# Third up projection wholly in seven products: its sums of weights formed earlier, and joint score visits for two more pairs

## The chip, the cores and the metric

The kernel runs on one core of a Trainium2 chip. The metric is the device time of one execution in microseconds. Before the change three runs gave 1011.73, 1011.96 and 1013.79 us; the median, 1011.96 us, is the number to compare with. Engines are called PE (TensorE, matmul), DVE (VectorE), ACT (ScalarE), POOL (GpSimd) and SP (SyncE, which here only issues DMAs).

## The reference

Sliding-window attention with a linear distance bias over 8 batches of 8 heads, 576 positions, 64 columns per head, then a bilinear feed-forward block over all 4608 tokens:

```
scores = q k^T / 8 - slope_h * |i - j|      (kept where 0 <= i - j < 128)
x      = softmax(scores) v                  (576 x 512 per batch)
out    = ((x w_a) * (x w_b)) w_out          (w_a, w_b: 512 x 1536, w_out: 1536 x 512)
```

All inputs are float32. The kernel forms most products from float16 pairs, a high and a low part, with three matmuls (high*high, high*low, low*high) per product.

## The kernel before

**Stages.** The work goes batch by batch. For each of the 8 batches there is an up projection (both w_a and w_b, and the product of the two) and a down projection (w_out). They are called here up 1, down 1, up 2, down 2, ... up 8, down 8; in the code batches count from 0, so up 3 belongs to `b == 2`. An up has twelve blocks of 128 hidden columns (`f` = 0..11), each for both halves of 288 tokens; a down has 2 halves by 4 blocks of output columns, each summed over the twelve `f`.

**Two ways of an up block.** `up_plain` needs 8 products per block, each of 6 matmuls of 288 columns: 48 matmuls. `up_fast` is a Strassen-like scheme with 7 products, 42 matmuls, but more additions: ACT copies and scales (L845, L857, L863), DVE adds and multiplies (L852, L868, L873, L880), and one multiplication on POOL (L875). It also needs other operands: sums and differences of the four weight quarters of a block (slots 3 to 6 of `wup[:, f]`), and sums of the four quarters of x (`split_x` with `fast`). Slot 3 is read by the plain way and overwritten by the sums, so a block's sums can only be formed once the last plain use of that block has been read.

**Sums of weights.** `sums_of_weights(f)` has two steps per block, 24 in all. A step is five POOL additions (L239 to L243), one ACT cast (L244) and one DVE subtraction (L245). Its two temporaries come from the pool of tiles `t` with 4 buffers, which the scores use as well. `ways` says which blocks of which batch are plain or fast, and `quota` lays the 24 steps along the matmul steps of ups and downs: `(8, 48, 6)` puts six of them evenly between step 8 and step 48 of that stage.

**Attention beside it.** While batch b goes through up and down, `attention()` works on the four head pairs of the following batch, a generator whose places (`yield i + k / 7`) are spread by `Pace` over the steps of up and down. `i` counts pairs, `p` is the pair in its batch. For a pair PE forms scores in four PSUM banks (`scores(o, bi)`: L362 float32 for the second batch, L366 float16 pairs later), DVE takes bias and minimum (L370), ACT the exponential (L371), ACT and DVE write normalised probabilities as high and low parts (L383, L384), a DMA transposes them (L389), and PE multiplies by v (L485). `two` says how many banks are formed in the pair's first visit. The next pair's q and k are loaded (L299, L300), squared on ACT (L309), scaled to a high part on ACT (L326) and a low part on DVE (L327), and laid out by four copies on the SP queue (L335 to L338). At `p == 1` the next v is loaded (L256) and squared on ACT (L265). At `p == 0` `split_x` splits the finished x of the batch into high and low parts (L419 on ACT, L420 on DVE), with four subtractions on POOL where the fast way is to be used (L433 to L443).

**What sets the order.** From up 2 on PE follows the order written in the program; DVE, ACT, POOL and the SP queue follow a scheduler that simulates the kernel while it is built and sets each engine's order by it. In up 1 and down 1 only SP keeps the written order, and PE is ordered by the scheduler too. Once built, every engine runs its list strictly in order: an instruction that waits holds up all behind it.

Of the kernel before, what the change touches and what calls it, by code (L numbers as in the profile page):

```python
# [21 lines left out]
B, H, S, D = 8, 8, 576, 64  # L22
# [24 lines left out]
def attention_then_bilinear_ffn(ctx: ExitStack, tc: tile.TileContext, qT, kT, vP, w_a, w_b, w_out, rel, slopes2, outT):  # L47
# [255 lines left out]
    def qk_squares(b, p, qk):  # L303
        o = State()
        o.b, o.p, o.qk = b, p, qk
        sums = small.tile([P, 1], F32, tag="qs", name="qs")
        hi = work.tile([P, 2, S], F16, tag="qkh", name="qkh", bufs=2)
        lo = work.tile([P, 2, S], F16, tag="qkl", name="qkl", bufs=2)
        act.activation(lo.bitcast(BF16), qk, AF.Square, accum_out=sums)  # L309

        o.both = small.tile([P, 2], BF16, tag="both", name="both")
        vec.tensor_scalar(out=o.both, in0=halves, scalar1=sums, scalar2=None, op0=ALU.mult)
        o.kh, o.kl = hi, lo
        return o

    def split_qk(o):

        b, p, qk, hi, lo = o.b, o.p, o.qk, o.kh, o.kl
        tot = ps_at.tile([P, 512], F32, tag="at", name="qtot")
        pe.matmul(tot[:, 0:2], ones16, o.both, start=True, stop=True)  # L320
        sc = small.tile([P, 2], F32, tag="sc", name="sc")
        power_scale(sc, tot[:, 0:2], 1.01, 15)
        own = small.tile([P, 3], F32, tag="own", name="own")
        vec.tensor_tensor_reduce(out=own[:, 0:2], in0=sc, in1=halves, scale=1.0, scalar=0.0, op0=ALU.mult, op1=ALU.add, accum_out=own[:, 2:3])
        own = own[:, 2:3]
        act.activation(hi, qk, AF.Copy, scale=own)  # L326
        vec.scalar_tensor_tensor(out=lo.rearrange("p h s -> p (h s)"), in0=qk.rearrange("p h s -> p (h s)"), scalar=own, in1=hi.rearrange("p h s -> p (h s)"), op0=ALU.mult, op1=ALU.subtract)  # L327
        o.sc = sc

    def lay_out_qk(o):  # L330


        b, p, hi, lo, sc = o.b, o.p, o.kh, o.kl, o.sc
        o.qs = work.tile([P, 2, S], F16, tag="qst", name="qst", bufs=1)
        sp.dma_start(o.qs[0:64, :, :], hi[0:64, :, :])  # L335
        sp.dma_start(o.qs[64:128, :, :], lo[0:64, :, :])
        sp.dma_start(hi[0:64, :, :], hi[64:128, :, :])
        sp.dma_start(lo[0:64, :, :], lo[64:128, :, :])  # L338

        t = small.tile([P, 1], F32, tag="ninv", name="ninv")  # L340
        vec.scalar_tensor_tensor(out=t, in0=sc[:, 0:1], scalar=-8.0, in1=sc[:, 1:2], op0=ALU.mult, op1=ALU.mult)
        o.neg = small.tile([P, 1], F32, tag="neg", name="neg")
        vec.reciprocal(o.neg, t)
        return t

    def before_scores(o, ninv):
        o.bias = work.tile([P, WIN], F32, tag="bias", name="bias")
        pool.tensor_scalar(out=o.bias, in0=rel_sb, scalar1=ninv, scalar2=sl2_sb[:, o.p:o.p + 1], op0=ALU.mult, op1=ALU.mult)  # L348
        o.mn, o.sm, o.rin = (small.tile([P, 9], F32, tag=tag, name=tag) for tag in ("mn", "sm", "rin"))
        o.n, o.parts = 0, []  # L350
# [67 lines left out]
    def split(n, src):  # L418
        act.copy(xs[:, n, 0, :, :], src)  # L419
        vec.tensor_tensor(out=xs[:, n, 1, :, :], in0=src, in1=xs[:, n, 0, :, :], op=ALU.subtract)  # L420

    def split_x(st, plain, fast):

        b11, b12, b21, b22 = (st.v[:, k:k + 2, t:t + HT] for k in (0, 2) for t in (0, HT))
        split(0, b11)
        if plain:
            split(1, b21)
            split(2, b22)
            split(B12, b12)
        if not fast:  # L430
            return
        yield
        pool.tensor_tensor(out=b11, in0=b12, in1=b11, op=ALU.subtract)  # L433
        if not plain:
            split(2, b22)
        pool.tensor_tensor(out=b12, in0=b22, in1=b12, op=ALU.subtract)
        split(4, b11)
        pool.tensor_tensor(out=b22, in0=b22, in1=b11, op=ALU.subtract)
        yield
        if not plain:  # L440
            split(1, b21)
        split(6, b12)
        pool.tensor_tensor(out=b21, in0=b21, in1=b22, op=ALU.subtract)  # L443
        yield
        split(5, b22)
        split(3, b21)
        yield
# [194 lines left out]
    def attention():  # L642


        n = NPAIR * (B - 1)
        qks = {}

        def load(i):
            if i < n:

                qks[i] = (load_plain_qk if i < NPAIR else load_qk)(1 + i // NPAIR, i % NPAIR)

        def squares(i):
            if i >= n:
                return None
            qk = qks.pop(i)
            return qk if i < NPAIR else qk_squares(1 + i // NPAIR, i % NPAIR, qk)

        def split(o):
            if o and o.b > 1:  # L660
                split_qk(o)

        def lay_out(o):
            if o:
                before_scores(o, lay_out_qk(o) if o.b > 1 else -8.0)

        def behind():

            return tc.issue_after(last_read[0].ins) if last_read[0] else ExitStack()

        load(0)
        st, prev = load_v(1), None
        o = squares(0)
        lay_out(o)
        load(1)
        yield 0
        for i in range(n + 1):
            b, p = 1 + i // NPAIR, i % NPAIR

            two = 2 if o and o.b >= 2 else 1  # L680
            for bi in range(two if o else 0):
                scores(o, bi)
            with behind():
                nxt = squares(i + 1)
            if p == 1 and b > 1:
                st = load_v(b)
            if p == 2:
                v_scale(st)
            yield i + 1 / 7
            if o and two == 1:  # L690
                scores(o, 1)

            if p == 2:

                with tc.issue_after(first_reads[0].ins) if first_reads[0] else ExitStack():
                    late.vhl = split_v(st, late.p)
            elif prev and p != 1:
                prev.vhl = split_v(st, prev.p)
            yield i + 2 / 7
            if p == 2:  # L700
                pv(late.p, st, late, late.vhl)
                transpose_probs(prev)
                split(nxt)
            if o and p != 2:
                with behind():
                    normalize(o)
            if p != 2:
                split(nxt)
            yield i + 3 / 7
            if o:  # L710
                scores(o, 2)
            if prev and p not in (1, 2):
                pv(prev.p, st, prev, prev.vhl)
            if two == 2 and p in (1, 3):
                if p == 2:
                    with behind():
                        normalize(o)
                scores(o, 3)
            yield i + 4 / 7
            if p == 2:  # L720
                prev.vhl = split_v(st, prev.p)
                if two == 1 or p not in (1, 3):
                    with behind():
                        normalize(o)
            if o and (two == 1 or p not in (1, 3)):
                scores(o, 3)
            lay_out(nxt)
            load(i + 2)
            if p == 1:
                v_squares(st, (0, 1))  # L730
            if prev and p == 0:
                states[b - 1] = st
                assert started["down"] == b - 2
                for k, _ in enumerate(split_x(st, b - 1 <= 2, b - 1 >= 2)):
                    yield i + (4.2 + 0.2 * k) / 7
            yield i + 5 / 7
            if o:
                with behind():
                    normalize(o)
            if p == 1:  # L740
                v_squares(st, (2, 3))
            yield i + 6 / 7
            if prev and p == 0:
                hidden_scale(st)
            if p == 2:
                pv(prev.p, st, prev, prev.vhl)
            if p == 1:
                late = prev
            elif o:
                transpose_probs(o)  # L750
            prev, o = o, nxt
            yield i + 1
# [221 lines left out]


    every = list(range(NF))
    ways = [(every, [])] * 2 + [(every[6:], every[:6])] + [([], every)] * (B - 3)
    att = Pace(attention())
    spread = chain.from_iterable(sums_of_weights(f) for f in every)

    quota = [((), ()), (((8, 48, 6),), ((0, 48, 4),)), (((0, 24, 2), (28, 66, 3)), ((0, 48, 3),)), (((0, 48, 6),), ())] + [((), ())] * (B - 4)

    def first_batch():
        st = states[0]
# [60 lines left out]
```

## Time and profile before

| | |
|---|---|
| time, median of 3 runs | 1011.96 us |
| the profiled execution: its own time / its span | 1013.37 us / 1011.6 us |
| PE busy | 969.4 us, 96% |
| DVE busy | 681.8 us, 67% |
| ACT busy | 643.0 us, 64% |
| POOL busy | 305.9 us, 30% |
| chain that ended last | PE 60%, DVE 12%, DMA 6%, ACT 6% |

Stages of the span, by the start of the first matmul of each: up 1 from 56 us, up 2 from 212.9, down 2 from 294.5, up 3 from 336.5, down 3 from 417.3, up 4 from 458.8, down 4 from 535.2, up 5 from 576.0, down 5 from 648.5, up 6 from 689.3 to 760.8 us.

How to read it: "busy" is the time in which an engine had an instruction under way. PE is pipelined, and a matmul of 288 columns stands in the trace with some 286 ns though one starts every 123 ns, so PE's idle time, and how long a stage takes, say more than its busy share. Idle time of an engine that PE doesn't wait for costs nothing.

### The profile page before, as it was taken

To read this page: it belongs to the slowest core of one execution; us is meant where nothing else is said; L and a number is where in the kernel's file an instruction comes from. 1 tells how busy PE (TensorE), PEld (TensorE's weight loads), DVE (VectorE), ACT (ScalarE), POOL (GpSimd) and SP (SyncE) were. 2 spreads that over 40 slices of the span, in tenths; PEclk is the share of its full clock that TensorE was granted. 3 is DMA by queue.
4 is the path that set the end of the run, shared out by engine and by line. 5 is a ranking of instruction groups with operands and counts; after the bars stand their busy time and mean duration, and the time that the engine had idled before them with its cause. 6 is when DMAs were issued, how large, how long until landed. Compare 5 with 4: busy or idle time off the path is not lost.

```text
span 1011.6 us, 23876 instructions
## 1 busy us (share of the span) xinstructions
PE 969.4 (96%) x9327; PEld 753.2 (74%) x9327; DVE 681.8 (67%) x1884; ACT 643.0 (64%) x1668; POOL 305.9 (30%) x347
## 2 busy tenths in 40 slices
PE   8789889999999999999899999999999999999998
PEld 6557666777777777776687777777777778777776
DVE  5988999567767666787776577766677576434430
ACT  6976779666666657667666776667667766423321
POOL 3533463001445313464724022221223022221100
PEclk9889999999999999999999999999999999999999
DMA  9307643574346242464424642464423632210001
GB/s 344 132 33 276 222 124 68 113 189 87 68 96 164 67 89 57 92 161 104 87 49 107 171 89 43 95 171 101 90 63 95 168 67 43 49 36 7 1 13 36
DMA packets 148433, 102.83 MB, mean 102 GB/s; under 512 B 120032, under 2 KB 128352, under 8 KB 147296
## 3 DMA queue, kind: packets, MB, share of 16 engines
q1 hardware_dynamic: 138816, 91.77, 37.0%
q10 hardware_dynamic: 9504, 9.54, 2.9%
q8 instruction: 73, 1.20, 0.5%
q14 instruction: 40, 0.33, 0.1%
HBM read 48.33 MB, written 9.44 MB: 57 GB/s over the span
## 4 chain that ended last, share of the span: by engine, by line
PE 60%; DVE 12%; DMA 6%; ACT 6%; issue 2%; POOL 2%; SPq 0%; ACTq 0%; DVEq 0%; POOLq 0%
PE ch L820 16%; PE dn_ps L916 16%; PE p L820 12%; PE up_ps L820 11%; PE x_ps L485 3%; DMA v<-in_vP 3%; DVE phl L384 3%; PE sc_ps L366 2%; ACT t L371 2%; DVE xs L420 1%; DMA qk<-in_kT 1%; DVE t L370 1%; ACT phl L383 1%; POOL wup L135 1%; DMA qst<-qkl 1%
## 5 line engine op out<-in xcount | busy, mean ns | idle before, releaser
L820 PEld LDWEIGHTS <-wup 128*128 128x128 f16 x4212 | 407.8, 98 | 126.7 <-issue 20.5
L916 PE MATMUL dn_ps<-h,wdn 128*128 128x288 f16 x2016 | 254.0, 286 | 0.1
L820 PE MATMUL ch<-xs,wup 128*128 128x288 f16 x1584 | 228.2, 286 | 7.1 <-DVE rc L880 4.2
L916 PEld LDWEIGHTS <-wdn 128*128 128x128 f16 x2016 | 193.9, 98 | 52.1 <-issue 0.3
L820 PE MATMUL up_ps<-xs,wup 128*128 128x288 f16 x1440 | 184.8, 288 | 6.2 <-DVE rc L769 4.6
L820 PE MATMUL p<-xs,wup 128*128 128x288 f16 x1188 | 178.0, 286 | 1.1 <-ACT rc L863 1.1
L875 POOL TENSOR_TENSOR rc<-rc,row 128x288 f32<-128x288 f32 x66 | 63.8, 966 | 241.2 <-DVE row L873 223.7
L371 ACT ACTIVATE t<-t,mn 128x192 f32<-128x192 f32 (+2 forms) x252 | 107.1, 427 | 33.3 <-DVE mn L370 33.2
L384 DVE SCALAR_TENSOR_TENSOR phl<-t,rin,phl 128x192 f16<-128x192 f32 (+2 forms) x252 | 104.6, 451 | 29.1 <-ACT phl L383 28.8
L813 ACT CAST h<-rc 128x576 f16<-128x576 f32 x96 | 64.2, 669 | 64.6 <-DVE rc L880 31.9
L383 ACT ACTIVATE phl<-t,rin 128x192 f16<-128x192 f32 (+2 forms) x252 | 88.5, 426 | 16.4 <-DMA pT<-phl 10.9
L814 DVE TENSOR_TENSOR h<-rc,h 128x576 f16<-128x576 f32 x90 | 73.4, 815 | 28.8 <-ACT h L813 28.2
L370 DVE CUSTOM_DVE_ANT_0 t<-sc_ps,bias,neg 128x192 f32<-128x192 f32 (+2 forms) x216 | 73.7, 390 | 8.6 <-PE sc_ps L366 8.6
L420 DVE TENSOR_TENSOR xs<-v,xs 128x576 f16<-128x576 f32 x51 | 52.1, 1032 | 28.6 <-ACT xs L419 28.1
L857 ACT ACTIVATE row<-ch,g 128x288 f32<-128x288 f32 x66 | 32.9, 498 | 58.1 <-PE ch L820 58.1
L135 POOL TENSOR_TENSOR wup<-wup,wdn 128x512 int32<-128x512 int32 x36 | 54.6, 1537 | 44.2 <-DVE wup L133 14.1
L921 ACT ACTIVATE row<-dn_ps,oi 128x288 f32<-128x288 f32 x56 | 27.8, 496 | 60.5 <-PE dn_ps L916 59.9
L852 DVE TENSOR_TENSOR rc<-p,rc 128x288 f32<-128x288 f32 x66 | 30.0, 454 | 44.9 <-PE p L820 34.8
L239 POOL TENSOR_TENSOR wa<-wup 128x512 f32<-128x512 f16 x24 | 30.5, 1270 | 64.8 <-DVE phl L384 40.2
L348 POOL TENSOR_SCALAR bias<-rel_sb,ninv,sl_sb 128x192 f32<-128x192 f32 x24 | 18.0, 751 | 102.6 <-DVE mn L370 96.8
L880 DVE SCALAR_TENSOR_TENSOR rc<-rc,g,ch 128x288 f32<-128x288 f32 x66 | 33.6, 509 | 22.6 <-PE ch L820 22.5
L414 POOL TENSOR_TENSOR xq<-xq,sq 128x576 bf16<-128x576 bf16 x22 | 31.3, 1424 | 54.8 <-ACT sq L413 54.4
(143 smaller groups left out, 1334.0 us busy)
## 6 DMA issues: line engine op xcount, KB each, us to landing
v<-in_vP SPq DMA_DIRECT2D x8, 1280.0 KB, 6.9
out<-row ACTq DMA_DIRECT2D x60, 144.0 KB, 2.0
qk<-in_qT SPq DMA_DIRECT2D x28, 288.0 KB, 3.9
qk<-in_kT SPq DMA_DIRECT2D x28, 288.0 KB, 4.4
wdn<-in_w_a SPq DMA_DIRECT2D x12, 512.0 KB, 4.5
wdn<-in_w_b SPq DMA_DIRECT2D x12, 512.0 KB, 5.4
wdn<-in_w_out SPq DMA_DIRECT2D x12, 512.0 KB, 4.4
qst<-qkh SPq DMA_DIRECT2D x24, 144.0 KB, 2.5
```

The source lines that it names most:

```text
L135: pool.tensor_tensor(out=t[:, m, :], in0=t[:, m, :], in1=low[:, m, :], op=ALU.add)
L370: vec.tensor_tensor_reduce(out=t[:, c:c + w], in0=ps[:, c:c + w], in1=o.bias[:, WIN - w:WIN], scale=-0.125 if o.b == 1 else o.neg, scalar= ...
L371: act.activation(t[:, c:c + w], t[:, c:c + w], AF.Exp, bias=o.mn[:, n:n + 1], scale=-1.0, accum_out=o.sm[:, n:n + 1])
L383: act.activation(phl[:, 0, pc:pc + w], e, AF.Copy, scale=s)
L384: vec.scalar_tensor_tensor(out=phl[:, 1, pc:pc + w], in0=e, scalar=s, in1=phl[:, 0, pc:pc + w], op0=ALU.mult, op1=ALU.subtract)
L420: vec.tensor_tensor(out=xs[:, n, 1, :, :], in0=src, in1=xs[:, n, 0, :, :], op=ALU.subtract)
L813: act.copy(h[:, f, :, 0, :], hid)
L814: eng.tensor_tensor(out=h[:, f, :, 1, :], in0=hid, in1=h[:, f, :, 0, :], op=ALU.subtract)
L820: pe.matmul(ps[:, 0:HT], wup[:, a[0], a[1], wi, k, :], xs[:, b, xi, k, :], start=(first and n == 0), stop=(last and n == len(ks) - 1), ski ...
L875: pool.tensor_tensor(out=x0, in0=x0, in1=mid, op=ALU.mult)
L880: vec.scalar_tensor_tensor(out=x1, in0=x1, scalar=st.g, in1=ch, op0=ALU.mult, op1=ALU.mult)
L916: pe.matmul(ps[:, 0:HT], wdn[:, f, wi, e * P:(e + 1) * P], h[:, f, t, hi, :], start=(m == 0 and n == 0), stop=(m == NF - 1 and n == 2))
```

## The change

Three places. In `attention`, `two` becomes 2 for pairs 2 and 3 of the second batch as well (`o.p > 1`), so that the first two score banks are formed in one visit and, for pair 3, the fourth bank with the third. `split_x` no longer makes the operands of the plain way for the third batch. And the third batch has all twelve blocks fast (before: six plain, then six fast), with the 24 steps of sums of weights moved: 11 in up 2, 6 in down 2, 7 in the first 60 of up 3's 84 steps, none later (before: 6 in up 2, 4 in down 2, 5 in up 3, 3 in down 3, 6 in up 4).

```diff
-            two = 2 if o and o.b >= 2 else 1
+            two = 2 if o and (o.b >= 2 or o.p > 1) else 1
...
-                for k, _ in enumerate(split_x(st, b - 1 <= 2, b - 1 >= 2)):
+                for k, _ in enumerate(split_x(st, b - 1 < 2, b - 1 >= 2)):
...
-    ways = [(every, [])] * 2 + [(every[6:], every[:6])] + [([], every)] * (B - 3)
+    ways = [(every, [])] * 2 + [([], every)] * (B - 2)
...
-    quota = [((), ()), (((8, 48, 6),), ((0, 48, 4),)), (((0, 24, 2), (28, 66, 3)), ((0, 48, 3),)), (((0, 48, 6),), ())] + [((), ())] * (B - 4)
+    quota = [((), ()), (((5, 48, 11),), ((0, 48, 6),)), (((0, 60, 7),), ())] + [((), ())] + [((), ())] * (B - 4)
```

On PE, in up 1, the scores of pair 2 of the second batch (`qkl`, `qkh` are the tiles that hold its plain q and k, `vtot` the sum of squares of v). The piece of the difference where its first bank stands:

```order
 L362 MATMUL sc_ps<-qkl,qkh 64x64 x2
 L362 MATMUL sc_ps<-qkl,qkh 64x128 x2
-L362 MATMUL sc_ps<-qkl,qkh 64x192 x2
+L362 MATMUL sc_ps<-qkl,qkh 64x192 x6
 L272 LDWEIGHTS ones_73
```

The four matmuls of the second bank now stand with the first; before they stood 24 matmuls of L820 further down. For pair 3 the first and second bank still stand apart, since the scheduler orders PE here.

On the SP queue, at the end of down 2, the copies that lay out the pair whose scores open up 3 (`qkh`, `qkl` copied onto their own lower halves are the last two) and the loads of the next pair. Before:

```order
L335 DMA qst<-qkh 64x1152
L336 DMA qst<-qkl 64x1152
L299 DMA qk<-in_qT 64x2x576
L337 DMA qkh<-qkh 64x1152
L338 DMA qkl<-qkl 64x1152
L300 DMA qk<-in_kT 64x2x576
```

After:

```order
L335 DMA qst<-qkh 64x1152
L336 DMA qst<-qkl 64x1152
L337 DMA qkh<-qkh 64x1152
L299 DMA qk<-in_qT 64x2x576
L338 DMA qkl<-qkl 64x1152
L300 DMA qk<-in_kT 64x2x576
```

The load of q has moved behind one of the two copies, not behind both.

On ACT, at the end of down 3, the squares of v (L265, which need the v load) and the high part of q and k for the pair whose scores open up 4 (L326). Before:

```order
L922 DMA out<-row 128x288
L265 ACTIVATE vsq,vs<-v 128x640
L326 ACTIVATE qkh<-qk,own 128x1152
L265 ACTIVATE vsq,vs<-v 128x640 x2
L921 ACTIVATE row<-dn_ps,oi 128x288
```

After:

```order
L922 DMA out<-row 128x288
L326 ACTIVATE qkh<-qk,own 128x1152
L265 ACTIVATE vsq,vs<-v 128x640 x3
L371 ACTIVATE t,sm<-t,mn 128x192
L921 ACTIVATE row<-dn_ps,oi 128x288
```

L326 no longer stands behind a square that waits for v. At the end of down 2 the order stays square first, then L326.

## Rows read from the trace of the kernel before

**Rows 1.** Busy time of each engine by stage, clock and DMA after it

```profile
core 0: us, PE busy (x) PEld busy (x) DVE busy (x) ACT busy (x) POOL busy (x), PEclk, DMA share, GB/s
56.00:168.90 112.90, 97.88 (x895) 72.86 (x891) 102.48 (x213) 86.17 (x193) 50.97 (x46) 0.97 0.46 145
...
212.90:294.50 81.60, 80.63 (x800) 63.63 (x799) 59.34 (x174) 57.24 (x156) 24.43 (x36) 1.00 0.50 111
294.50:336.50 42.00, 41.17 (x408) 32.04 (x406) 30.98 (x94) 29.08 (x83) 21.09 (x23) 1.00 0.47 122
336.50:417.30 80.80, 77.53 (x747) 60.31 (x745) 55.49 (x147) 50.81 (x130) 28.49 (x40) 0.98 0.35 73
417.30:458.80 41.50, 41.22 (x409) 32.08 (x407) 31.01 (x97) 29.15 (x83) 18.49 (x22) 1.00 0.56 139
458.80:535.20 76.40, 71.62 (x709) 55.97 (x709) 60.48 (x157) 52.98 (x135) 35.43 (x46) 1.00 0.38 81
535.20:576.00 40.80, 40.80 (x408) 31.98 (x406) 24.89 (x94) 27.04 (x78) 9.12 (x7) 1.00 0.57 144
576.00:648.50 72.50, 71.25 (x711) 55.90 (x709) 52.63 (x151) 49.93 (x130) 16.22 (x16) 1.00 0.38 76
...
689.30:760.80 71.50, 70.93 (x711) 55.92 (x709) 51.45 (x148) 48.51 (x125) 16.14 (x16) 1.00 0.38 78
```

**Rows 2.** PE's longest waits in up 3: total us, times, longest

```profile
PE sc_ps L366 <- DMA qkh<-qkh: 1.7, 1, 1.7
...
PE sc_ps L366 <- DMA qkl<-qkl: 0.2, 1, 0.2
```

**Rows 3.** PE's two largest waits in up 4, same view

```profile
PE ch L820 <- DVE rc L880: 2.6, 2, 1.6
PE p L820 <- ACT rc L863: 1.1, 1, 1.1
```

**Rows 4.** Timeline of up 4, all engines: start us, us, instruction [idle before <-releaser]

```profile
487.88 1.67 POOL L239 TENSOR_TENSOR wa<-wup 128x512 f32<-128x512 f16 x1
...
488.82 1.27 DVE L245 TENSOR_TENSOR wup<-ws,wup 128x512 f16<-128x512 f32 x1
...
490.01 0.50 DVE L880 SCALAR_TENSOR_TENSOR rc<-rc,g,ch 128x288 f32<-128x288 f32 x1
...
490.57 0.90 PE L820 MATMUL ch<-xs,wup 128*128 128x288 f16 x6 [1.61 <-DVE rc L880]
```

**Rows 5.** Timeline across the start of up 3, SP queue and PE

```profile
333.52 0.66 SPq L299 DMA_DIRECT2D qk<-in_qT  x1
334.27 0.57 SPq L337 DMA_DIRECT2D qkh<-qkh  x1
335.76 0.46 SPq L338 DMA_DIRECT2D qkl<-qkl  x1
...
336.50 1.63 PE L820 MATMUL up_ps<-xs,wup 128*128 128x288 f16 x12
...
340.24 0.22 PE L366 MATMUL sc_ps<-qkl,qst 128*64 128x64 f16 x2 [0.16 <-DMA qkl<-qkl]
```

**Rows 6.** Stages' view of 3 us after that wait, columns as in rows 1

```profile
341.00:344.00 3.00, 3.00 (x19) 2.01 (x18) 2.06 (x11) 2.51 (x8) 1.74 (x4) 0.54 0.14 49
```

**Rows 7.** PE's timeline: runs of matmuls in up 2 and up 3

```profile
219.04 14.87 PE L820 MATMUL up_ps<-xs,wup 128*128 128x288 f16 x120
...
341.12 15.06 PE L820 MATMUL up_ps<-xs,wup 128*128 128x288 f16 x108
```

**Rows 8.** POOL's additions in up 2, then L245 ns min/median/max

```profile
212.90:294.50 81.60, 19.83 (x30) 1.00 0.50 111
...
L245 DVE TENSOR_TENSOR wup<-ws,wup x24: 660/692/1635, 240.9 to 506.8; 128x512 f16<-128x512 f32 x24
```

**Rows 9.** PE's waits in up 1 between 100 and 168 us

```profile
PE up_ps L820 <- DVE rc L769: 4.6, 2, 2.3
...
PE x_ps L485 <- DVE vhl L284: 1.5, 1, 1.5
```

## The prediction

> **What bounds the kernel now.** I read the busy times by stage first. From up 2 on PE is the bound: in up 5 it is busy 71.25 of 72.5 us, in down 4 all of 40.8 [rows 1]. What a stage costs is therefore its matmuls plus what PE idles, and three idle times matter. Up 3 idles 80.8 - 77.53 = 3.3 us, up 4 idles 76.4 - 71.62 = 4.8, up 5 only 1.25 [rows 1]. Up 4 and up 5 do the same work but for the six steps of sums of weights in up 4; up 6 is like up 5. Only up 1 is different: DVE is busy 102.48 of 112.9 us there while PE idles 15 [rows 1]. I then asked PE's waits what the idle is. In up 3, 1.9 us is one wait at its start, for the copies of q and k [rows 2]; the other 1.4 is spread. In up 4 two causes take 3.7: DVE's L880 and ACT's L863 come late [rows 3]. The timeline shows how for the largest: L245, a sum's subtraction, takes 1.27 us while POOL adds, L880 stands behind it on DVE and starts at 490.01, and PE has waited 1.61 us when it ends [rows 4]. So sums cost time where the fast way runs; the plain way of up 2, with six steps of them too, idles 81.6 - 80.63 = 1.0 us in all [rows 1].
>
> **Matmuls removed.** Six blocks go from 48 to 42 matmuls: 36 fewer, in up 3. A run of 120 took 14.87 us with the last one's 0.29 in it whole, so about 0.123 each [rows 7]: 36 x 0.123 = 4.4 us off PE, which is the bound there. -4.4.
>
> **Sums and fast blocks in up 3.** Seven steps now stand in 60 of 84 matmul steps (one per 8.6), and the whole stage is fast, as up 4 was with six in 48 (one per 8.0). I carry up 4's 3.7 us over in the ratio of the rates, 3.7 x 8.0/8.6 = 3.5, in place of the 1.4 that up 3 spreads now: +2.1. Bounds: 0 (three sums in the fast half of up 3 now fit into its 1.4, and up 5 idles 1.25 with none) and +3.4 (all of up 4's 4.8 in place of 1.4).
>
> **The start of up 3.** The pair's scores wait for the copy of `qkl`, issued at 335.76, behind a load of q issued at 333.52; PE has done 12 matmuls of the plain first product at 338.13 (336.50 + 1.63) and stands until 340.24 [rows 5]. In the fast order the scores stand behind 6 matmuls, 0.7 us sooner. On the queue the load moves behind the `qkh` copy but stays ahead of `qkl`, and on ACT the high part still stands behind the first square of v. So I expect the wait to stay, with 0.7 us more: +0.7. What follows the wait belongs to its price: in the next 3 us the granted clock is 0.54, so partly at 1.2 instead of 2.4 GHz [rows 6], and 108 matmuls took 15.06 us instead of some 13.3 [rows 7], 1.8 us. This is in the time before and I leave it in. Bounds: -3.7 (wait and low clock both gone) to +3 (the two more sums of down 2 push L326 back by as much as a sum's 3.3 us on POOL, 19.83/6 [rows 8]). Up 3 in all: -4.4 + 2.1 + 0.7 = -1.6.
>
> **Up 4 and down 3 lose their sums.** Up 4 becomes what up 5 and up 6 are: 76.4 -> (72.5 + 71.5)/2 = 72.0 [rows 1], -4.4. On ACT at the end of down 3 the high part of q and k now stands ahead of the squares of v, so the start of up 4 waits for no v load either. Down 3 becomes down 4: 41.5 -> 40.8, -0.7 [rows 1]. These two are the surest terms: from there on all engines have the order of the stages that follow, whose times stand in the trace.
>
> **Down 2** gets six steps instead of four and one split of x less. Four cost 42.0 - 40.8 = 1.2 against a down without, 0.3 each [rows 1]: two more +0.6, less a little for the split: +0.4 (0 to +1).
>
> **Up 2** gets 11 steps instead of 6. What hides them is the slack of the plain way: DVE has 22 us free of 81.6, POOL 57 [rows 1]. Five L245 at 0.69 us are 3.5 us of DVE and five steps 16.5 us of POOL [rows 8]. If a step cost PE what it costs in up 4, 3.7/6 = 0.6, they would take +3; if all are hidden, 0. I take +0.5, near what six do now.
>
> **The joint visits** lie in up 1 and down 1, where DVE sets the pace: their order moves, no DVE work is added. The wait for `vhl`, 1.5 us, now has 24 more matmuls ahead of it and may go; another wait like the 2.3 us for L769 may come [rows 9]. I take 0, bounds -1.5 and +2.3. Pair 3's first visit is not joint in PE's order, so there only the order changes.
>
> **A rule that speaks against it.** The Trainium skill, "SBUF — State Buffer", section "Who interferes with whom", says that a DVE instruction with two SBUF inputs and a GpSimd instruction that reads SBUF exclude each other for the whole instruction. The trace agrees in the one L245 of 1.27 us under a POOL addition, though the median of 24 is 0.69 against a shortest of 0.66. By that rule taken at its full weight in up 2 the sum would be that of the slower rival below.
>
> **The sum.** -1.6 - 4.4 - 0.7 + 0.4 + 0.5 + 0 = -5.8. Against the profiled span of 1011.6 us this is 1005.8, against that execution's own time of 1013.37 it is 1007.6. That execution was 1.4 us above the median of the runs; I put the sum on the median: 1011.96 - 5.8 = 1006.2. Its own range is 1003.5 to 1008.7.
>
> **Rivals.**
> - *The start of up 3 comes free.* The queue reorder lets the copies land before PE gets there, or down 2 runs ahead. For it: the q load no longer stands ahead of `qkh`; the wait is only 1.9 us. Against: `qkl` still has the load ahead, and PE comes sooner. Then +0.7 becomes -3.7: 1006.2 - 4.4 = 1001.8.
> - *Sums eat what up 3 saves.* Up 3 gets all bounds on the high side (+3.4 instead of +2.1, +2 instead of +0.7 at the start), up 2's five cost +2: -5.8 + 1.3 + 1.3 + 1.5 = -1.7, 1010.3. For it: up 4 shows the price. Against: its six steps stood closer.
> - *DVE becomes the bound in up 2 (slower than before).* Each of the five steps holds POOL 3.3 us; if DVE is shut out for all of that, DVE goes from 59.34 to 59.34 + 3.5 + 16.5 = 79.3 of 81.6 us. It decides from the share at which up 1 runs, 102.48/112.9 = 91%, 74 us: there PE idles 13% [rows 1]. 13% of 81.6 is 10.6 us: -5.8 - 0.5 + 10.6 = +4.3, 1016.3. For it: a L245 of up to 1.6 us [rows 8]. Against: that share needs over 2 us shut out per step, and up 2 idles 1.0 us with six of them.
> - *The change doesn't do what it says.* PE's list has 36 matmuls and 36 weight loads fewer, so this has no chance for the ups; for pair 3's joint visit it is so, at no price.
>
> **How the numbers follow.** Forecast 0.53, free start 0.23, eaten 0.16, DVE-bound 0.08. A measurement of this kernel tells about 0.2%, 2.0 us, from no change: faster means below 1009.9. The forecast and the free start lie there whole (0.76), and half of the eaten case, whose terms are at their bounds (0.08): 0.84 faster. The other half and a slice of the DVE case that is only partly reached make 0.09 the same, 0.07 slower. The range takes in the free start and the eaten case to near its middle: 1001.5 to 1010.0.
>
> **What would show it.** Right: up 4 near 72 us with PE idle near 1; down 3 at 40.8; up 3 near 79, with a wait of 2 to 3 us for `qkl` some 0.7 us into it and a granted clock well under 1 after that; L880 or L863 late while L245 runs; up 2 within 1 us of 81.6. Wrong: up 2 longer by several us with DVE above 90%; PE waiting for a weight load of the last blocks in up 3, whose sums are placed latest; a low clock in new places of up 3; or up 1 and down 1, which no matmul left, moving by over 2 us.

## The result: slower by 0.3%

The changed kernel takes 1014.93 us (median of 11 runs, 1011.13 to 1016.86), the kernel before, run beside it, 1011.57 us (11 runs, 1010.48 to 1013.79). The ratio is 1.0031, 95% interval 1.0022 to 1.0040: 3.1 us slower. Forecast were 1006.2 us and a range up to 1010.0. The profiled execution took 1015.75 us with a span of 1014.0, 2.4 us more than that of before.

Single executions of one kernel lie up to 6 us apart, so below the ratio of the runs says how much, and the stages of the one profiled execution say where. Stage lengths in us, by the first matmul of each stage (of up 1, the first L820, which stands at 57.27 us before, not at 56):

| stage | before | after | difference | predicted |
|---|---|---|---|---|
| up 1 + down 1 | 155.67 | 157.09 | +1.4 | 0 |
| up 2 | 81.56 | 88.21 | **+6.65** | +0.5 |
| down 2 | 42.00 | 42.41 | +0.4 | +0.4 |
| up 3 | 80.79 | 78.59 | -2.2 | -1.6 |
| down 3 | 41.48 | 40.84 | -0.6 | -0.7 |
| up 4 | 76.40 | 73.26 | -3.1 | -4.4 |
| down 4 to down 7 | 375.8 | 375.3 | -0.5 | 0 |

Most of the miss is up 2. The stage windows of the kernel after, columns as in [rows 1]: up 1, down 1, up 2, down 2, up 3, up 4.

```profile
57.65:167.09 109.44, 96.21 (x869) 71.69 (x867) 97.47 (x196) 82.73 (x188) 49.38 (x45) 0.97 0.46 150
167.09:214.74 47.65, 44.48 (x459) 34.09 (x457) 30.55 (x103) 29.93 (x84) 7.69 (x7) 1.00 0.58 123
214.74:302.95 88.21, 83.75 (x800) 65.05 (x798) 68.60 (x178) 59.60 (x160) 43.29 (x60) 0.96 0.45 102
302.95:345.36 42.41, 41.07 (x408) 32.04 (x406) 31.75 (x98) 29.91 (x84) 28.37 (x33) 1.00 0.45 117
345.36:423.95 78.59, 72.93 (x710) 56.64 (x708) 62.35 (x159) 54.32 (x138) 40.90 (x55) 0.98 0.38 82
...
464.79:538.05 73.26, 71.21 (x710) 55.88 (x708) 52.78 (x152) 50.72 (x133) 15.84 (x16) 1.00 0.37 75
```

In up 2, where [rows 1] have DVE at 59.34 of 81.60 us, DVE is now busy 68.60 us for four more instructions, and the mean clock is 0.96. PE's waits of after, in down 1, up 2 and up 3 (total us, times, longest), answering to [rows 2] and [rows 3]:

```profile
PE x_ps L485 <- DMA pT<-phl: 1.9, 1, 1.9
PE dn_ps L796 <- ACT row L806: 1.2, 1, 1.2
...
PE sc_ps L366 <- DVE mn L370: 3.7, 1, 3.7
...
PE ch L820 <- DVE rc L880: 3.8, 2, 2.0
PE sc_ps L366 <- DMA qkl<-qkl: 1.8, 1, 1.8
```

One wait of 3.7 us stands in up 2; before, the same wait was 0.3 us. The timeline of after around it:

```profile
267.20 0.22 PE L366 MATMUL sc_ps<-qkh,qst 128*64 128x64 f16 x2
...
267.66 0.69 DVE L245 TENSOR_TENSOR wup<-ws,wup 128x512 f16<-128x512 f32 x1 [1.53 <-ACT wup L244]
...
270.28 0.28 DVE L370 CUSTOM_DVE_ANT_0 t<-sc_ps,bias,neg 128x64 f32<-128x64 f32 x1
...
274.03 2.83 DVE L384 SCALAR_TENSOR_TENSOR phl<-t,rin,phl 128x64 f16<-128x64 f32 x5
...
277.20 0.93 DVE L245 TENSOR_TENSOR wup<-ws,wup 128x512 f16<-128x512 f32 x1
...
279.05 0.27 PE L366 MATMUL sc_ps<-qkh,qst 128*64 128x192 f16 x2
...
279.13 1.10 DVE L245 TENSOR_TENSOR wup<-ws,wup 128x512 f16<-128x512 f32 x1 [1.00 <-ACT wup L244]
...
282.84 1.42 DVE L327 SCALAR_TENSOR_TENSOR qkl<-qk,own,qkh 128x1152 f16<-128x1152 f32 x1 [0.21 <-ACT qkh L326]
284.18 0.41 DVE L370 CUSTOM_DVE_ANT_0 t<-sc_ps,bias,neg 128x192 f32<-128x192 f32 x1
...
284.99 0.37 PE L366 MATMUL sc_ps<-qkh,qst 128*64 128x192 f16 x2 [3.72 <-DVE mn L370]
...
285.77 11.46 PE L820 MATMUL up_ps<-xs,wup 128*128 128x288 f16 x72
```

And the same place before:

```profile
265.82 0.22 PE L366 MATMUL sc_ps<-qkh,qst 128*64 128x64 f16 x2
...
266.39 0.28 DVE L370 CUSTOM_DVE_ANT_0 t<-sc_ps,bias,neg 128x64 f32<-128x64 f32 x1 [1.35 <-PE sc_ps L366]
...
270.29 1.53 DVE L384 SCALAR_TENSOR_TENSOR phl<-t,rin,phl 128x64 f16<-128x64 f32 x5
...
277.03 0.27 PE L366 MATMUL sc_ps<-qkh,qst 128*64 128x192 f16 x2
...
278.52 0.41 DVE L370 CUSTOM_DVE_ANT_0 t<-sc_ps,bias,neg 128x192 f32<-128x192 f32 x1
...
279.33 0.27 PE L366 MATMUL sc_ps<-qkh,qst 128*64 128x192 f16 x2 [0.32 <-DVE mn L370]
```

PE forms a bank of scores, multiplies another pair by v (which takes two more PSUM banks of the three), and can go on only when DVE's L370 has read the first bank. Before, L370 starts 1.5 us after the scores; after, 5.1 us. DVE falls behind in steps before that. Counted from the pair's first scores (265.82 us before, 267.20 after), its first L370 comes 0.6 us later in the kernel before and 3.1 us later in the changed one: ahead of it stands a L245 that had waited 1.5 us for ACT's cast, and L284 behind that. Then the same five L384 take 2.83 instead of 1.53 us. Between them and the L370 that PE waits for stand two L245 (one before), the second after another 1.0 us of waiting for its cast. At that L370 DVE is 4.3 us later than before, by the same count. Then the clock; windows of 3 us from 283.74 of after, columns as in [rows 1]:

```profile
283.74:286.74 3.00, 1.75 (x13) 1.12 (x14) 1.96 (x9) 2.05 (x8) 0.00 (x0) 0.55 0.31 86
286.74:289.74 3.00, 3.00 (x14) 1.93 (x13) 1.34 (x2) 1.30 (x6) 2.98 (x5) 0.50 0.89 210
289.74:292.74 3.00, 3.00 (x22) 2.19 (x20) 1.28 (x5) 2.94 (x7) 0.46 (x1) 0.82 0.26 61
```

After the stop the granted clock is 0.50 to 0.55, the 1.2 GHz level. The run of 72 matmuls behind it takes 11.46 us where the rate of [rows 7] gives 71 x 0.1225 + 0.29 = 9.0. So 3.4 us more of waiting (3.72 against 0.32) and 2.5 us of low clock make 5.9 of the 6.65.

Where DVE's time went shows in its groups in up 2 (xcount | busy us, mean ns). Before:

```profile
L384 DVE SCALAR_TENSOR_TENSOR phl<-t,rin,phl 128x192 f16<-128x192 f32 x21 | 9.1, 484 | 0.1
...
L245 DVE TENSOR_TENSOR wup<-ws,wup 128x512 f16<-128x512 f32 x6 | 5.0, 832 | 1.0 <-ACT wup L244 1.0
```

After:

```profile
L384 DVE SCALAR_TENSOR_TENSOR phl<-t,rin,phl 128x192 f16<-128x192 f32 x21 | 12.8, 665 | 0.0
...
L245 DVE TENSOR_TENSOR wup<-ws,wup 128x512 f16<-128x512 f32 x11 | 9.5, 860 | 4.5 <-ACT wup L244 4.4
```

Five more L245 are 4.5 us, and the same 21 L384, which belong to no sum, have grown by 3.7 us. Besides, DVE stood idle 4.4 us in front of L245, for casts that ACT had not made yet, where it stood 1.0 before; since DVE keeps its order, all behind such a L245 waits too.

### The profile page after: what moved, and what is told of

It is laid out like the page before. It is cut to its first block, busy times and chain, and to the rows that moved or that the text cites. A ratio compares the mean times of both kernels' runs of the same rounds, so it can differ in the third digit from the quotient of the medians.

```text
span 1014.0 us, 23838 instructions
## 1 busy us (share of the span) xinstructions
PE 966.4 (95%) x9291; PEld 750.4 (74%) x9291; DVE 684.3 (67%) x1895; ACT 644.9 (64%) x1673; POOL 314.1 (31%) x353
## 4 chain that ended last, share of the span: by engine, by line
PE 53%; DVE 6%; DMA 5%; ACT 4%; issue 1%; POOL 0%; ACTq 0%; SPq 0%; DVEq 0%
PE ch L820 18%; PE dn_ps L916 16%; PE p L820 14%; PE x_ps L485 3%; PE sc_ps L366 2%; DMA v<-in_vP 2%; DVE phl L384 2%; ACT t L371 1%; DMA pT<-phl 1%; ACT phl L383 1%; DVE xs L420 1%; DVE qkl L327 1%; DVE t L370 1%; DVE h L814 1%; DVE rc L880 1%
## 5 line engine op out<-in xcount | busy, mean ns | idle before, releaser
L820 PEld LDWEIGHTS <-wup 128*128 128x128 f16 x4176 | 406.0, 98 | 126.3 <-issue 18.1
L820 PE MATMUL ch<-xs,wup 128*128 128x288 f16 x1728 | 249.5, 286 | 8.4 <-DVE rc L880 6.1
L820 PE MATMUL p<-xs,wup 128*128 128x288 f16 x1296 | 195.1, 287 | 0.0
L820 PE MATMUL up_ps<-xs,wup 128*128 128x288 f16 x1152 | 150.7, 291 | 4.7 <-DVE rc L769 3.4
L875 POOL TENSOR_TENSOR rc<-rc,row 128x288 f32<-128x288 f32 x72 | 69.3, 963 | 271.2 <-DVE row L873 260.4
L384 DVE SCALAR_TENSOR_TENSOR phl<-t,rin,phl 128x192 f16<-128x192 f32 (+2 forms) x252 | 104.9, 450 | 33.4 <-ACT phl L383 33.3
L857 ACT ACTIVATE row<-ch,g 128x288 f32<-128x288 f32 x72 | 35.9, 498 | 65.5 <-PE ch L820 65.5
L370 DVE CUSTOM_DVE_ANT_0 t<-sc_ps,bias,neg 128x192 f32<-128x192 f32 (+2 forms) x216 | 73.9, 389 | 4.5 <-PE sc_ps L366 4.5
L852 DVE TENSOR_TENSOR rc<-p,rc 128x288 f32<-128x288 f32 x72 | 32.7, 454 | 44.2 <-PE p L820 31.5
L880 DVE SCALAR_TENSOR_TENSOR rc<-rc,g,ch 128x288 f32<-128x288 f32 x72 | 36.6, 509 | 25.2 <-PE ch L820 25.2
L485 PE MATMUL x_ps<-pT,vhl 128*64 128x128 f16 (+3 forms) x1176 | 46.3, 229 | 3.6 <-DMA pT<-phl 1.9
L485 PEld LDWEIGHTS <-vhl 128*64 128x64 f16 (+1 forms) x1176 | 42.8, 109 | 9.0 <-issue 5.9
```

Of the source, the lines that this page charges most:

```text
L370: vec.tensor_tensor_reduce(out=t[:, c:c + w], in0=ps[:, c:c + w], in1=o.bias[:, WIN - w:WIN], scale=-0.125 if o.b == 1 else o.neg, scalar= ...
L384: vec.scalar_tensor_tensor(out=phl[:, 1, pc:pc + w], in0=e, scalar=s, in1=phl[:, 0, pc:pc + w], op0=ALU.mult, op1=ALU.subtract)
L485: pe.matmul(xp[oc // 512][64 * h:64 * h + 64, o0:o0 + w], vt[0:rows, c:c + 64], probs(pt, rows, blocks, h), start=(n == 0 and first), stop ...
L820: pe.matmul(ps[:, 0:HT], wup[:, a[0], a[1], wi, k, :], xs[:, b, xi, k, :], start=(first and n == 0), stop=(last and n == len(ks) - 1), ski ...
L875: pool.tensor_tensor(out=x0, in0=x0, in1=mid, op=ALU.mult)
```

## The experiments

Each was run with the kernel before on the same chip; ratios are to that. Stage lengths and waits are those of one profiled execution of each kernel. Some edits shift the lines of the code below them by up to six.

### Which part of the change: sums or visits

Theory A: the sums in up 2 crowd DVE there. Theory B: the joint visits shift the attention into them. Four kernels, one part undone or kept each.

**Without the joint visits**

```diff
-two = 2 if o and (o.b >= 2 or o.p > 1) else 1
+two = 2 if o and o.b >= 2 else 1
```

> The changed kernel without the joint visits (two as before), everything else of the change kept. Theory A (the eleven sums in up 2 fill DVE in one place, PE waits there and runs at the low clock afterwards; the joint visits cost only what up 1 and down 1 show together, 1.5 us): up 2 stays near 88 us, time about 1014.9 - 1.5 = 1013.5 us. Theory B (the joint visits shift the attention, and the sums only meet it at a bad place for that reason): up 2 falls back to about 82 us, time about 1014.9 - 1.5 - 6.5 = 1007 us.

Measured: 1014.08 us, ratio 1.0013 (1.0005 to 1.0022). Up 2 of this kernel:

```profile
212.61:300.78 88.17, 83.33 (x800) 64.89 (x797) 69.19 (x182) 59.50 (x160) 43.23 (x60) 0.96 0.46 104
```

Its wait for L370:

```profile
PE sc_ps L366 <- DVE mn L370: 3.7, 1, 3.7
```

The same 88.2 us and the same wait: B falls. By the two ratios the joint visits cost about 1.8 us of the 3.1.

In up 3 PE waits 1.8 us for `qkl` in the changed kernel and in this one. The 3 us behind that wait, in the changed kernel, then in this one:

```profile
348.40:351.40 3.00, 3.00 (x32) 1.98 (x29) 2.52 (x13) 2.30 (x4) 2.23 (x5) 0.58 0.24 77
...
346.20:349.20 3.00, 2.86 (x38) 2.16 (x37) 2.44 (x12) 2.59 (x6) 2.27 (x4) 1.00 0.23 74
```

The granted clock is 0.58 there and 1.00 here, so an equal stop is not always followed by the low clock; why is not shown.

**The joint visits alone**, the same line in the kernel before.

> The kernel before with the joint visits alone. Theory A: up 1 and down 1 together 1.5 us longer, up 2 as before at 81.6 us, time about 1011.6 + 1.5 = 1013 us. Theory B: up 2 is longer too, by several us even with six sums; with the whole 6.6 us the time is about 1019.5 us.

Measured: 1015.05 us, ratio 1.0024 (1.0014 to 1.0035). Up 1, down 1 and up 2:

```profile
58.32:167.78 109.46, 96.35 (x870) 71.82 (x868) 97.42 (x197) 82.70 (x188) 49.39 (x45) 0.97 0.47 150
167.78:215.51 47.73, 44.46 (x458) 34.08 (x456) 30.27 (x102) 29.94 (x84) 7.67 (x7) 1.00 0.58 122
215.51:296.98 81.47, 80.58 (x800) 63.60 (x797) 59.12 (x174) 57.23 (x156) 24.84 (x36) 1.00 0.50 111
```

Up 2 is untouched, as A says; up 1 and down 1 together are 1.5 us longer than before, with the waits for `pT` (1.9 us) and L806 (1.3 us) in down 1. The other kernels say the same: these two stages take 156.6 to 157.4 us in all eight that have both joint visits, and 154.5 to 155.7 in the nine without that of pair 2.

**Six sums in up 2**, more later

```diff
-quota = [((), ()), (((5, 48, 11),), ((0, 48, 6),)), (((0, 60, 7),), ())] ...
+quota = [((), ()), (((8, 48, 6),), ((0, 48, 8),)), (((0, 60, 10),), ())] ...
```

> The changed kernel, joint visits included, with 6 steps of sums in up 2 (as before), 8 in down 2 and 10 in the first 60 steps of up 3, in place of 11, 6 and 7. Theory A: up 2 back to 81.6 us, down 2 0.6 us and up 3 1.5 us longer than in the changed kernel (three more steps at some 0.5): about 1014.9 - 6.6 + 2.1 = 1010.4 us. Theory B: up 2 stays near 88 us, time about 1014.9 + 2.1 = 1017 us.

Measured: 1017.08 us, ratio 1.0047 (1.0034 to 1.0059). Up 2, down 2, up 3:

```profile
216.18:297.83 81.65, 80.58 (x799) 63.60 (x797) 59.04 (x175) 56.71 (x155) 24.42 (x36) 1.00 0.49 111
297.83:342.81 44.98, 42.69 (x408) 32.83 (x406) 34.45 (x100) 31.44 (x88) 31.98 (x39) 0.96 0.47 118
342.81:428.39 85.58, 73.94 (x710) 56.68 (x708) 68.21 (x161) 55.33 (x139) 54.62 (x75) 0.98 0.34 71
```

Up 2 is back, as A said, but its price for the moved steps was wrong: down 2 is 2.6 us longer than in the changed kernel, not 0.6, and up 3 7.0, not 1.5. PE's waits for L880 in up 3 are 7.4 us there, against 3.8 in the changed kernel.

**Six sums and no joint visits**, both edits.

> Both edits: sums 6, 8 and 10 in up 2, down 2 and up 3, and no joint visits. Theory A: 1010.4 - 1.5 = 1008.9 us, about 2.7 us under the kernel before. Theory B: about 1007 + 2.1 = 1009.1 us, so this one doesn't tell them apart; it shows whether a wholly fast third up is worth anything by itself.

Measured: 1016.39 us, ratio 1.0038 (1.0024 to 1.0051), 7 us off the expectation, for the same reason: up 2 81.9, up 3 86.7 us.

### What in a sum costs the time

Theory C: DVE's own subtraction. Theory D: POOL's additions read SBUF and keep DVE from reading meanwhile. Theory E: a sum holds two of the four tiles `t` that the scores need. Theory F: POOL's length alone.

**No subtraction**

```diff
-vec.tensor_tensor(out=wup[:, f, 3:7, 1, k, :], in0=z, in1=wup[:, f, 3:7, 0, k, :], op=ALU.subtract)
+vec.memset(wup[:, f, 3:7, 1, k, :], 0.0)
```

The kernel leaves the low part of the sums out; DVE still writes it, as zeros.

> The changed kernel; in every sum of weights DVE's subtraction L245 is left out, and the low part of the sums is set to zero on DVE instead (the low part is left out of the result). POOL's five additions and ACT's cast stay. Theory C (DVE's own work for the sums, two L245 with their wait for the cast, 3 us in the place where L370 comes late, makes PE stop): up 2 falls from 88.2 to about 82.5 us, up 3 from 78.6 to about 77, time about 1014.9 - 7 = 1008 us. Theory D (POOL's additions keep DVE from its ports and stretch L384 and others; L245 itself is small): L384 keeps its mean of 0.66 us in up 2, up 2 stays above 86 us, time about 1013 us or more.

Measured: 1009.44 us, ratio 0.9967 (0.9956 to 0.9978). Up 2 is 82.9 us as C says, up 3 stays at 78.5, against C's 77. L384 is shorter, but still 586 ns:

```profile
L384 DVE SCALAR_TENSOR_TENSOR phl<-t,rin,phl 128x192 f16<-128x192 f32 x21 | 11.3, 586 | 0.1
...
L245 DVE MEMSET wup<- 128x256 uint32 x11 | 3.0, 272 | 0.6 <-POOL wa L239 0.6
```

The edit takes two things from DVE at once: the subtraction (9.5 us became 3.0) and the wait for ACT's cast in front of it (4.4 us, now none). Which of them counts for more is not shown. PE's wait for L370 is down to 1.1 us.

**No additions**

```diff
-a, z = ...            # two tiles t
-pool.tensor_tensor(...)   # five of them
+z = sl2_sb[:, 0:4].unsqueeze(2).to_broadcast([P, 4, P])
```

The kernel leaves the sums out, and so do the next two.

> The changed kernel; in every sum of weights POOL's five additions are left out (cast and subtraction read a constant instead, so the sums are left out of the result), and no tile t is taken for them. Theory D: L384 falls back from 0.66 to 0.48 us in up 2 and L245 from 0.86 to 0.66, up 2 to about 82 us, up 3 to about 76.5, time about 1014.9 - 8 = 1007 us. Theory C: DVE still has eleven L245, up 2 stays above 86 us, time about 1012 us or more. If both show up 2 near 82 us, the two have to come together.

Measured: 1002.52 us, ratio 0.9894 (0.9877 to 0.9910). Nothing paces a sum now, and 23 of the 24 came to stand in up 2. That stage, with its L245 (here L239) and L384 (L378):

```profile
216.08:297.53 81.45, 80.51 (x800) 63.60 (x798) 65.11 (x193) 65.66 (x173) 5.64 (x6) 1.00 0.50 112
```

```profile
L239 DVE TENSOR_TENSOR wup<-sl_sb,wup 128x512 f16<-128x512 f32 x23 | 16.2, 720 | 1.7 <-ACT wup L238 1.4
...
L378 DVE SCALAR_TENSOR_TENSOR phl<-t,rin,phl 128x192 f16<-128x192 f32 x21 | 7.6, 414 | 0.1
```

Twenty-three subtractions, 16.2 us of DVE, and PE loses nothing in 81.45 us. So DVE's own work for the sums is not enough to stop PE; in up 2 of the changed kernel it takes both. Without the subtraction the stage is 5.3 us shorter, without the additions 6.8.

**The tiles without the additions**

```diff
-pool.tensor_tensor(out=a, in0=..., in1=..., op=ALU.add)
+pool.memset(a, 0.0)
...                         # likewise the four parts of z
```

> The changed kernel; POOL's five additions of a sum become five settings to zero of the same shapes in the same two tiles t, so that the tiles are taken and released as before but POOL reads nothing for the sums (the sums are left out of the result; cast and subtraction stay). Theory D (POOL's reading additions keep DVE out): as without any POOL work, L384 back at 0.41 to 0.48 us, up 2 about 82 us, up 3 72 to 74, time about 1003 to 1005 us. Theory E (the two tiles t held by each sum make the scores late): up 2 stays above 85 us or up 3 above 77, time 1009 us or more.

Measured: 1004.36 us, ratio 0.9916 (0.9903 to 0.9930); up 2 81.4, up 3 74.2 us, L384 415 ns, with eleven L245 in up 2. The tiles are taken as in the changed kernel: E falls as the cause in up 2. But a sum holds POOL, and with it the tiles, for a shorter time here, 1.2 us from its first setting to the end of its last; additions that nothing holds up take some 3.0.

**The same with POOL held longer**: eleven settings to zero in a sum.

```diff
+pool.memset(a, 0.0)        # a twice, z's parts twice, the first three times
```

> As the run with zeros in both tiles, but eleven settings to zero in each sum instead of five, so that POOL is held for about 2.9 us in each as by the additions (two or three for each tile part: 0.52 and 0.20 us apiece); the sums are left out of the result. Theory D (what hurts is that POOL's additions read SBUF and keep DVE out): still no stretch, L384 at 0.41 to 0.45 us, up 2 81.4 to 82, up 3 under 75.5, time 1004 to 1006.5 us. Theory F (what hurts is that a sum takes POOL over 3 us, so that its tiles and its DVE step come late): up 2 or up 3 go back towards 88 and 78.6 us, time 1009 us or more, with L384 short all the same.

Measured: 1002.11 us, ratio 0.9892 (0.9875 to 0.9909). Up 2 and up 3, then DVE's groups in up 2 (L384 is L390 here, L245 is L251):

```profile
216.29:297.60 81.31, 80.68 (x799) 63.60 (x797) 58.06 (x178) 59.33 (x160) 31.04 (x127) 1.00 0.49 111
...
338.43:411.08 72.65, 71.36 (x710) 55.86 (x708) 57.38 (x157) 52.56 (x135) 33.14 (x93) 1.00 0.38 81
```

```profile
L390 DVE SCALAR_TENSOR_TENSOR phl<-t,rin,phl 128x192 f16<-128x192 f32 x21 | 7.7, 417 | 0.0
L251 DVE TENSOR_TENSOR wup<-ws,wup 128x512 f16<-128x512 f32 x11 | 7.5, 684 | 1.3 <-ACT wup L250 1.3
```

As many L245 and the same tiles, and a sum holds POOL for 2.6 us, close to the 3.0 of undisturbed additions, only without reading: L384 is 417 ns and the loss is gone. From 1.2 to 2.6 us of POOL per sum nothing was lost, so F has nothing for it, though a hold of the full 3 us was not run; D stands. Nor do the zeros in the weights make PE faster: up 5 to up 7, which multiply by them too, take 71.5 to 71.9 us here and 71.5 to 72.5 in the changed kernel. DVE in up 2 is busy 58.06 us against 68.60 in the changed kernel, so POOL's reads cost 10.5 us of DVE over eleven steps, 0.96 each, beside the 0.68 of L245 itself. DVE's waits for the cast fall with them, from 4.4 us to 1.3. Against the changed kernel the whole time is 1 - 0.9892/1.0031 = 1.4% less: about 14 us hung on these reads.

### One tile for a sum

**In place**

```diff
-a, z = ...                 # two tiles t, five additions
+z = work.tile([P, 4, P], F32, tag="t", name="ws32", bufs=4)
+pool.tensor_tensor(out=z[:, 1:4:2, :], in0=w0[:, 0:2, :], in1=w1[:, 0:2, :], op=ALU.add)
+pool.tensor_tensor(out=z[:, 0:3:2, :], in0=w0[:, 2:4, :], in1=w1[:, 2:4, :], op=ALU.add)
+...                        # the other four in z itself
```

> The changed kernel; each sum of weights is formed in place in one tile t instead of two (POOL then needs six additions instead of five, the result is the same). Theory E (the sums hold the tiles that the scores need, and the scores come late for that reason): up 2 falls to about 82 us and up 3 by 1 to 2 us, time about 1007 us. Theories C and D: DVE's and POOL's work is the same or a little more, up 2 stays near 88 us, time about 1015 us.

Measured: 1008.14 us, ratio 0.9959 (0.9946 to 0.9973). Both sides missed: up 2 gains only 2.4 us (85.8, its wait for L370 still 2.7 us), up 3 gains 4.0 (74.6). Of these 4.0 the start of up 3 makes 3.4: the wait of 1.8 us for `qkl` is gone, and PE's busy time, 72.93 us in the changed kernel with the low clock behind that wait, is 71.33. On ACT the high part of q and k (L326, here L327) now stands ahead of the squares of v. The waits for L880 fall from 3.8 to 2.5 us.

**In place in the kernel before**

> The kernel before, its ways, quota and visits unchanged, with each sum formed in place in one tile t by six additions. Theory E: up 3, down 3 and up 4, which carry most of its sums in the fast way, gain 1 to 2 us together, time 1010 us or less. Theory D: the extra addition (0.4 us of POOL in each of 24 steps) helps nothing, time 1012 us or more. It also tells how much of the gain of the one tile belongs to the change at all.

Measured: 1012.94 us, ratio 1.0002 (0.9993 to 1.0011): nothing there. So the gain belongs to the change, whose sums stand closer together. Why up 2 gains is not settled: L384 in up 2 is at 522 ns, so the additions meet less of DVE's work, but the edit changes the tiles, the additions and the scheduler's order at once.

**In place and no joint visits**

> The changed kernel with one tile per sum and without the joint visits, 11, 6 and 7 sums as there. The two effects add up: joint visits cost 1.5 to 2 us in up 1 and down 1, so about 1008.1 - 1.8 = 1006.3 us with up 2 still near 86 us (its wait of 2.7 us stays). If the joint visits move what meets the sums in up 2, up 2 differs from 85.8 by over 1 us.

Measured: 1006.88 us, ratio 0.9945 (0.9932 to 0.9958): 5.6 us faster than the kernel before and the fastest version that computes everything. Up 2 and up 3:

```profile
213.34:296.21 82.87, 80.59 (x799) 63.60 (x797) 64.07 (x177) 58.66 (x159) 44.67 (x71) 1.00 0.48 109
...
339.29:414.30 75.01, 71.39 (x711) 55.94 (x709) 62.55 (x158) 53.42 (x136) 40.84 (x61) 1.00 0.38 79
```

Up 2 differs by 2.9 us from the version with joint visits, so in these two executions the effects don't simply add up. One L246 fewer (ten) stands in the stage here, and PE's wait for L370 is 1.6 us instead of 2.7. The rest is the clock: PE is busy 80.59 us at a clock of 1.00 here, 82.25 us at 0.98 there.

### How many sums where, and which visit

**Nine, seven, eight, no joint visits**

```diff
-(((5, 48, 11),), ((0, 48, 6),)), (((0, 60, 7),), ())
+(((5, 48, 9),), ((0, 48, 7),)), (((0, 60, 8),), ())
```

> No joint visits, and 9, 7 and 8 steps of sums in up 2, down 2 and up 3 (changed kernel: 11, 6 and 7). If the price is one burst that crosses a threshold (Theory A with slack that nine steps still fit into): up 2 about 82 us, down 2 42.8, up 3 about 78.7, time about 1014.1 - 6.5 + 0.4 + 0.8 = 1008.8 us, faster than the kernel before. If every step beyond six costs the same (6.6/5 = 1.3 us in up 2, 2.3 us in up 3): up 2 about 85.5, up 3 about 80.2, time about 1014 us.

Measured: 1013.83 us, ratio 1.0006 (0.9997 to 1.0015). Up 2 has room for nine (82.0 us), the threshold that A needs; but one more step in up 3 makes it 83.9 instead of 77.9 us. With ten it was 86.7. So the price of a step comes in jumps: 6.1 us for the eighth, 1.4 each for the next two. **The same with one tile**:

> As the one before, but 9, 7 and 8 sums in up 2, down 2 and up 3. If up 2 has room for nine and one tile takes away what eight or more cost in up 3: up 2 about 82 us, down 2 43.4, up 3 about 76, time about 1006.3 - 3.8 + 0.9 + 1.4 = 1004.8 us. If the price only moves on with the sums, up 3 is 79 us or more and the time 1007.5 us or more.

Measured: 1009.55 us, ratio 0.9968 (0.9956 to 0.9981): up 2 81.2, up 3 80.6 us. The price moved on with the sums. **Eleven, eight, five with one tile**:

```diff
-(((5, 48, 11),), ((0, 48, 6),)), (((0, 60, 7),), ())
+(((5, 48, 11),), ((0, 48, 8),)), (((0, 50, 5),), ())
```

> The fastest version so far (one tile per sum, no joint visits) with 11, 8 and 5 sums in up 2, down 2 and up 3 instead of 11, 6 and 7. If a step costs less in a down than in a fast up: down 2 +0.6 us (two more at 0.3), up 3 from 75.0 to about 73.3, time about 1 us less, 1006 us. If the price of a step is the same where POOL's additions lie beside DVE's work: no change, 1006.9 us.

Measured: 1012.20 us, ratio 0.9995 (0.9985 to 1.0005). Missed: down 2 went from 43.1 to 47.0 us, with two new PE waits for DVE (2.3 us for L501, 1.9 for L815), and up 3 is longer with five than with seven (76.8 against 75.0, with a wait of 2.5 us for L858). Down 2 with eight steps took 45.0 and 43.3 us in the two kernels with six in up 2, so what a step costs in a down is not settled: it hangs on the order.

**The joint visit of pair 3 alone**, in the kernel before

```diff
-two = 2 if o and o.b >= 2 else 1
+two = 2 if o and (o.b >= 2 or o.p > 2) else 1
```

> The kernel before with the joint visit for pair 3 of the second batch alone. If pair 2's joint visit is what makes the transposed probabilities of pair 2 late in down 1 (PE's wait of 1.9 us), up 1 and down 1 stay at 111.9 and 43.8 us and the time is that of before. If pair 3's visit does it, down 1 is about 47 us and the time about 1.5 to 2.5 us above before.

Measured: 1012.46 us, ratio 0.9995 (0.9986 to 1.0005); down 1 43.7 us. It costs nothing, so pair 2's visit does, alone or with the other; pair 2 alone was not run. In the changed kernel pair 2's probabilities are transposed later although down 1 begins sooner, and PE runs out of other work:

```profile
173.00 4.82 SPq L389 DMA_TRANSPOSE pT<-phl  x1
...
179.84 1.62 PE L485 MATMUL x_ps<-pT,vhl 128*64 128x128 f16 x40 [1.93 <-DMA pT<-phl]
```

Before, this transposition was issued at 170.16, 1.0 us into down 1; now at 173.00, 5.9 us into it.

## Why the prediction was wrong

- **The step that failed is up 2**, "I take +0.5, near what six do now". Its bound of +3 came from up 4's price per step and was too low as well: it measured +6.65. The sentence before it, "DVE has 22 us free of 81.6", was true and the wrong reading: what counts is how soon after the scores DVE comes to L370. PE waited 0.3 us there already. One pair's work met three subtractions, two of which held DVE idle for their casts, and L384 stretched by POOL's additions; PE then waited 3.7 us. The stop cost the low clock on top, 2.5 us, which the prediction had priced in up 3 [rows 6] and not here. It also took L245 at 0.69 us, the median of all 24 [rows 8]; in up 2 their mean was 0.83 us before and is 0.86 now.
- **The slower rival had the right mechanism and the wrong point of decision.** It had DVE shut out by POOL's additions, asked for over 2 us a step and a share of 91%, and got a chance of 0.08. Measured are 0.96 us a step and a share of 68.60/88.21 = 78%; one crowded place was enough. The rule that it leaned on, in the Trainium skill, "SBUF — State Buffer", section "Who interferes with whom", also says that a POOL instruction that only writes does not contend with a DVE instruction with two SBUF inputs. The run with POOL held by zeros agrees: L384 417 ns, against 665 under the additions.
- **Joint visits**: 0, bounds up to +2.3. Measured +1.4 and +1.5 in the stages, 1.8 and 2.4 us in the ratios of the runs. That is at the upper bound, and the order that the scheduler gives to pair 2's probabilities had not been priced.
- **Matmuls removed and up 3**: -1.6 predicted, -2.2 measured, with L880 late (3.8 us) and the wait for `qkl` (1.8 us) where they were expected: right. PE idles 5.7 us there, 1.8 and 3.8 in these two; predicted were 2.6 (1.9 + 0.7) and 3.5. Without POOL's reads up 3 is 72.65 us, 5.9 less. But 3.4 of that is the start, the wait for `qkl` and the low clock behind it, which are gone there (PE busy 71.36 us against 72.93); at the sums themselves L880's waits fall from 3.8 to 1.3 us.
- **Down 2** (+0.4) and **down 3** (-0.6 against -0.7) were right. **Up 4** gave back 3.1 of 4.4 us in this execution; in the kernels whose up 3 is changed it lies between 72.1 and 73.4 us, against the predicted 72.0.
- The quota was the hidden premise: the 24 sums have to be done a stage earlier, by the end of up 3 instead of up 4. Up 2 took nine at almost no cost (82.0 and 81.2 us), but then up 3 lost 6 us to its eighth step; with eleven in up 2 it was up 2 that lost. Either is more than the 4.4 us that the 36 matmuls save. Only with the sums formed in place was a split of all 24 faster than the kernel before (up 2 82.9 and up 3 75.0 us in the fastest).

## What to carry to other kernels

Price an instruction of POOL that reads SBUF by what it does to DVE's instructions beside it, and take that from the stretch of a DVE group that has nothing to do with the change. Slack is not a stage's free time but the time between a producer and the one consumer that PE will wait for; look for the place where the new work meets it, and look for a low clock behind each stop of PE. It isn't always there: behind the 3.7 us it cost 2.5 us, behind the 1.6 us in up 2 of the fastest version nothing, and behind the 1.8 us for `qkl` in up 3 the granted clock was 0.58 in the changed kernel and 1.00 in the one without joint visits. Work that has to be done earlier needs room in the earlier stage, and the price of filling that room can come all at once, with one piece more.

## What was not expected of the hardware

DVE instructions far shorter than POOL's can pay for the whole of it. In up 2 of the changed kernel one L113, 128 x 2 int32 with a single input, took 1.16 us beside a POOL addition of 1.16 us; three of them in up 2 of the kernel before average 155 ns. A second case is one L379 of 128 x 4, 1.16 us beside L414, where two before average 171 ns. The first:

```profile
247.34 1.16 POOL L239 TENSOR_TENSOR wa<-wup 128x512 f32<-128x512 f16 x1 [1.45 <-DVE cl L107]
...
247.37 1.16 DVE L113 TENSOR_SCALAR r<-cl 128x2 int32<-128x2 int32 x1
```

POOL is held up by DVE in turn: with eleven settings to zero its sums' instructions keep 205 and 523 ns, while an addition of 128 x 128 takes 0.46 us alone and up to 1.57 us in up 2. That longest one, an L241 from 224.84 us, stands beside a DVE L327 of 1.55 us that began at 224.54.
